# A new order table, engine table and buffer table for a hand-scheduled attention + MoE kernel

## The chip, the cores and the metric

One core of a Trainium2 chip runs the whole program; the metric is device microseconds of that core, the median of several runs. Its engines take instructions from queues of their own, in order, and wait for each other through semaphores: TensorE (PE in the rows, its weight loads PEld), VectorE (DVE), ScalarE (ACT), GpSimd (POOL) and SyncE (SP), whose queue issues all the kernel's DMAs.

## The reference

```python
# q, k, v: (4, 8, 1152, 64) float32; w_in (512, 2048), w_out (2048, 512)
q_pool = q.reshape(B, H, S // 2, 2, D).mean(axis=3)           # 576 queries
scores = (1.0 / np.sqrt(D)) * np.matmul(q_pool, k.transpose(0, 1, 3, 2))
scores = scores - np.max(scores, axis=-1, keepdims=True)
attn = np.exp(scores)
attn = attn / (np.sum(attn, axis=-1, keepdims=True) + 1e-09)
x = np.matmul(attn, v)        # then transposed to (B * 576, 8 * 64) = (2304, 512)
h = x @ w_in
g = np.where(h > 0.0, h, np.exp(np.minimum(h, 0.0)) - 1.0)
out = g @ w_out               # (2304, 512) float32
```

## The kernel before

There are four units of work, one for each batch. In a unit, attention goes over four pairs of heads; each pair has nine steps of 128 queries (four for each head, and one that takes the last 64 queries of both). Numbers that must be exact are split into a high and a low float16 part (`hi`, `lo`), so most products are done as three matmul passes.

One attention step is this chain, each link a task: `scores` (TensorE, L890, L895, L904, into the single score buffer `s` in PSUM); `biggest` (VectorE, L919: scales `s` into a buffer `ep` and takes the extreme of each row); `expo` (ScalarE, L925); `recip` (the row sum's reciprocal); then one of two ways to the transposed weights `pT`. In the 45 steps of unit 0 and of one more pair: `norm_pool` normalises in `ep` (POOL L945, DVE L948 or ACT L951), TensorE transposes (`turn`, L1002) and `out_act` copies to `pT` (ACT L1012, DVE L1015). In the other 99 steps: `phi_act` makes the high half in a buffer `hb` (ACT L973 or POOL L970), `plo` the low half in `ep` (DVE L976), and two DMA transposes (`p_turn`, L982) put both into `pT`. Then `pv` or `pv_split` (TensorE, L1034, L1046) multiplies with V, and `xb` copies the result to `x32` (DVE L1059 and L1061, ACT L1055).

Before a pair's steps come its loads (L586 to L598), `q_sum` (L607, adds the two queries that are pooled, on DVE or POOL), sums of absolute values (ACT L545), a scale, `hi` (ACT L551 or POOL L502) and `lo` (DVE L565 or POOL), and DMA transposes of Q and K (L647, L698). The weights are loaded and decoded through unit 0 (`dec`, DVE L776 to L780; `w_hi`, `w_lo` L803 to L812).

The MoE part of a unit runs in two groups of 256 and 320 tokens: `m1_all` (TensorE L1149), `neg` and `ex` (ACT L1162, L1165), `em` (POOL L1170, ACT L1175 or DVE L1180), `join` (DVE L1185), `gh` (ACT L1199 or POOL L1207), `gl` (POOL L1203 or DVE L1211), `m2_all` (TensorE L1231), `oe` (ACT L1247) and the store. The MoE of one unit is woven into the attention of the next.

All 2788 tasks are first listed; then two tables written out as text say everything about their order. A word of `ORDER` is a task's number and the letter of its engine (p, v, a, g for PE, DVE, ACT, POOL; s for a DMA on SP); instructions are emitted in that order, so it fixes the order on each engine's queue. `SLOTS` gives, for each buffer in turn, which pool and which place in it. Pools that matter here: `s` 1, `ep` 4 (5 more live in `w_out` space in unit 0), `hb` 2, `pT` 2. Waits follow from the order and the buffers. A score step uses TensorE's array whole and then split by rows, `pv` splits it by columns; `Plan.run` turns a score step round when the array is not whole:

```python
for word in ORDER.split():
    t = self.tasks[int(word[:-1])]
    t.eng = engines[word[-1]]
    t.dur, t.emit = t.ways[t.eng]
    if t.eng == "PE":
        if t.modes == ("full", "row") and mode != "full":
            t.modes, t.turned = ("row", "full"), True
        mode = t.modes[1]
    order.append(t)
```

Of the kernel before, what the change touches and what calls it, by code (L numbers as in the profile page):

```python
# [32 lines left out]
0s 1g 2a 3s 5a 6p 7v 8p 9v 343s 344s 369s 349s 354s 23a 345v 10a 12g 24v 11v 371v 35s 31p 33p 29p  # L33
346v 32a 34a 30a 13p 25p 36g 14a 472p 347a 26a 27p 28a 15p 16a 38s 21p 473v 425s 338s 474a 40a 22a
19p 485p 351v 486v 475g 496p 364s 356v 487a 37a 476a 17p 41p 497v 488g 20a 461p 353s 359s 18a 498a
481p 42v 340v 374s 4s 462v 489a 43p 427v 477p 463a 44v 339s 520p 499g 490p 464g 465g 500a 521v 482a
366v 494p 491a 495a 522a 557p 348s 479p 523g 466p 45a 467a 470p 471a 478a 558v 46v 544p 545v 480v
47s 524a 529p 527p 559a 492p 501p 509p 468p 560v 502v 528a 50g 51g 510v 546a 561a 503p 53s 533p
525p 469a 511a 504a 505p 547g 483p 48s 350v 52s 493a 506a 512v 513a 534v 341v 361v 376v 562p 530a
514p 49s 618p 526a 518p 56s 535a 515a 563a 352a 368s 548a 58a 536v 507p 54g 55a 508a 551p 564p 565a  # L40
420s 537g 540p 516p 552a 619v 355v 519a 517a 541a 59p 60v 553p 357a 342a 61p 363s 542p 370v 543a
62v 620a 581p 549p 566p 582v 538p 567v 484a 539a 554a 372a 63g 570p 64v 571v 568p 605p 583a 550v
555p 572a 429s 621v 584v 606v 585a 358s 68g 69g 622g 573v 574a 360v 627p 628a 65s 373s 556a 586p
# [36 lines left out]
2004g 1009a 986s 1983p 155s 1001a 1016v 1023p 977p 2016v 458v 459a 460g 978a 1002v 995p 1003s 2024g  # L80
1004s 1024v 150a 1033p 2041a 2042a 1025a 1026g 1027g 1011s 151v 1010v 2010a 156s 1017a 1012s 2047p
1034v 2043g 1978p 1984p 157a 996a 1018v 2044v 1019a 1035a 2017a 2025g 1028v 1041p 158a 154a 1036v
1042v 2018g 1979a 146s 1021s 1013p 1051p 1014a 1985a 1030s 159p 1020v 2011v 1043a 1029s 1980s 2045g
1044g 1045g 1986s 1022s 160v 2026p 161p 162v 1052v 1037a 2027a 2028a 163a 2096p 2048a 1039s 168a
2029a 1995v 1038v 2049a 2050a 2046g 1047s 164v 2075p 1069p 1070v 1040s 1053a 1031p 2051v 2030v 169g
1061p 1054v 173s 165s 1071a 1032a 1055a 1046v 1048s 2061p 2054p 1062v 2110p 1057s 2031g 2032v 1056v
2076a 2055a 2056a 2077a 2057g 2058v 1087p 1072v 2062a 1063a 2063a 1088v 2064a 1058s 166s 1049p 170s
2052g 2059g 2060g 1064v 1050v 2097a 2098a 1079p 167s 2082p 2099a 2100v 2065v 2078g 1073g 2068p
2053g 2111p 2066a 2101g 1080v 2102g 1074v 1065a 1067s 1089a 1097p 1059p 1076s 1066v 1075s 1090v
1068s 2069a 2070a 1081a 2083a 2084a 2071g 2072v 1082v 2079v 1098v 2067g 1091a 1093s 176s 2073g  # L90
2080g 2081v 2085g 1060v 171g 1092v 2089p 1083a 1105p 1106v 2122p 2123p 1077p 2090a 1123p 2086v
1107a 2091a 2092a 1085s 1094s 1099a 1108g 1109g 1084v 172v 2103p 2087g 2074g 2112p 1110v 1124v
1115p 2104a 2105a 2093v 2106g 1100v 174g 1086s 2107v 1078v 178a 2108g 2109g 177s 1111s 1101a 1095p
1116v 1102v 1112s 1103s 1117a 1118g 1133p 179a 1119g 2116p 1134v 2094g 2095g 1096a 2128v 1104s
1135a 1125a 1141p 1120v 1126v 1121s 1122s 2088g 1142v 1127a 1113p 175a 2124p 1128v 1136v 1129s
1143a 1137a 1130s 1159p 1139s 1160v 1138v 1114a 1144g 1145a 1146v 1161a 1162g 1163g 2117p 1140s
1131p 1132a 2129v 1151p 180p 2130v 1152v 1148s 181v 1147s 1153a 1164v 2113p 2114a 182p 2131p 2132v
183v 1166s 1187p 1188v 2133p 184g 185v 2134v 1165s 2125p 2115s 1154g 1155g 189a 2137a 1169p 1149p
1170v 2138v 1171a 186s 187s 1179p 1172g 1173g 1156v 1158s 1175s 1157s 1180v 1174v 2153p 2139p 1181a
1150a 2126a 2140a 190v 188s 1176s 1182v 2135v 2141a 2142v 2181p 2143v 2154a 1197p 1167p 1189a 1198v  # L100
2144g 1190g 2145g 1191g 2155a 2156v 2157v 1177p 1168v 1205p 1206v 2127s 191s 194s 2182a 1183a 1192v
2136v 1184v 1178v 1207a 1199a 2183a 2184a 2185v 1200v 1208v 192g 1194s 2167p 1185s 2160p 1233p
2158g 2161a 2162a 2168a 195g 1234v 1193s 2174p 1186s 2163a 2164v 1209a 2169a 1210v 2159g 1201a
# [1200 lines left out]
```

## Time and profile before

| what | value |
|---|---|
| median of 3 runs | 794.65 us (794.53 to 795.88) |
| the profiled execution | 793.59 us, its span 791.5 us, so 2.1 us lie around the span |
| TensorE, VectorE, ScalarE, GpSimd busy | 723.1, 642.9, 585.0, 377.7 us |
| mean granted TensorE clock | 0.990 |

The span runs from the first to the last instruction of the program. A busy TensorE is one with a matmul in the array; the time between matmuls that the page counts as busy can still hold short pauses. "A <- B" in a wait means that an instruction of A stood until one of B had ended.

### The profile page before, as it was taken

Reading aid. Unit: us, or ns where it says so; the run is one execution under the profiler, and the core shown is the slowest. Engines: PE = TensorE matmul, PEld = TensorE weight load, DVE = VectorE, ACT = ScalarE, POOL = GpSimd, SP = SyncE. Lnnn points to the kernel's source line nnn. Section 1 sums busy time; section 2 is a strip of 40 time slices with the busy share of each in tenths; the row PEclk is TensorE's granted clock in tenths of the full one; section 3 lists DMA queues with packets and bytes.
Section 4 is the critical chain, followed back from the end, with each engine's and each line's share of the span. In section 5 each row is a group of like instructions: output and inputs, shape, how many; then the busy total and the mean of one; then the engine's idle time right before and its main releaser. Section 6 shows DMA issues by size and latency. Waiting matters only on the chain. (4 is left out here: it accounts for less than half of the span.)

```text
span 791.5 us, 19657 instructions
## 1 busy us (share of the span) xinstructions
PE 723.1 (91%) x7845; PEld 477.0 (60%) x7845; DVE 642.9 (81%) x1147; ACT 585.0 (74%) x987; POOL 377.7 (48%) x411
## 2 busy tenths in 40 slices
PE   2777898999998989999999899998999988999997
PEld 1455666777565655775556565776665545785653
DVE  4999999999997769898889888899797978875330
ACT  3899999999897867577677666878679755682551
POOL 1344455278655745363475463656346344152230
PEclk9699999999999999999999999999999999999999
DMA  6788763718999999997999797699899999655001
GB/s 212 282 230 201 221 195 111 181 32 168 180 193 207 190 189 179 175 202 135 215 200 202 136 221 147 145 172 169 178 173 209 175 187 149 133 98 99 14 1 33
DMA packets 315819, 129.39 MB, mean 163 GB/s; under 512 B 290064, under 2 KB 292112, under 8 KB 315728
## 3 DMA queue, kind: packets, MB, share of 16 engines
q1 hardware_dynamic: 315728, 128.15, 78.7%
q8 instruction: 61, 1.00, 0.5%
q14 instruction: 30, 0.25, 0.1%
HBM read 45.09 MB, written 4.72 MB: 63 GB/s over the span
## 5 line engine op out<-in xcount | busy, mean ns | idle before, releaser
L919 DVE TENSOR_SCALAR_CACHE_REDUCE ep<-s,sm 128x1152 f32<-128x1152 f32 x139 | 196.1, 1411 | 32.2 <-DMA pT<-ep 20.2
L925 ACT ACTIVATE ep<-ep,wk 128x1152 f32<-128x1152 f32 x139 | 174.2, 1254 | 48.4 <-DVE ep L919 36.3
L1149 PE MATMUL r<-x,wi 128*128 128x256 f16 (+1 forms) x1536 | 197.0, 286 | 0.8 <-DVE tmp L1185 0.8
L1231 PE MATMUL r<-wo,g 128*128 128x512 f16 (+1 forms) x864 | 175.6, 380 | 2.5 <-POOL g L1203 2.2
L1149 PEld LDWEIGHTS <-wi 128*128 128x128 f16 x1536 | 147.8, 98 | 41.3 <-issue 4.2
L976 DVE SCALAR_TENSOR_TENSOR ep<-ep,wk,hb 128x1152 f16<-128x1152 f32 x99 | 150.0, 1521 | 16.0 <-POOL hb L970 8.5
L1231 PEld LDWEIGHTS <-g 128*128 128x128 f16 (+1 forms) x864 | 74.2, 100 | 84.4 <-POOL g L1203 3.1
L890 PE MATMUL s<-kT,qT 128*128 128x512 f16 (+3 forms) x480 | 97.0, 334 | 25.2 <-DVE ep L919 16.4
L1046 PE MATMUL r<-pT,v 128*64 128x128 f16 (+1 forms) x2970 | 85.1, 215 | 4.4 <-DMA pT<-ep 3.1
L1046 PEld LDWEIGHTS <-v 128*64 128x64 f16 x2970 | 78.0, 110 | 15.7 <-issue 14.2
L973 ACT ACTIVATE hb<-ep,wk 128x1152 f16<-128x1152 f32 x51 | 63.7, 1252 | 31.6 <-DMA pT<-hb 15.0
L1203 POOL TENSOR_TENSOR g<-tmp,g 128x320 f16<-128x320 f32 (+1 forms) x63 | 67.2, 1072 | 36.7 <-ACT g L1199 35.1
L970 POOL TENSOR_SCALAR hb<-ep,wk 128x1152 f16<-128x1152 f32 x48 | 61.8, 1288 | 45.1 <-DVE wk L934 16.4
L890 PEld LDWEIGHTS <-qT 128*128 128x128 f16 (+1 forms) x480 | 39.2, 101 | 66.9 <-issue 37.6
L1162 ACT ACTIVATE tmp<-r 128x320 f32<-128x320 f32 (+1 forms) x96 | 45.9, 479 | 36.5 <-PE r L1149 34.7
L502 POOL TENSOR_SCALAR wk<-wk 128x1 f32<-128x1 f32 x59 | 23.1, 391 | 102.1 <-ACT ep L925 98.1
L1185 DVE SCALAR_TENSOR_TENSOR tmp<-r,tmp 128x320 f32<-128x320 f32 (+1 forms) x96 | 51.9, 550 | 21.9 <-POOL tmp L1170 15.9
L904 PE MATMUL s<-kT,qT 64*128 64x512 f16 (+1 forms) x320 | 57.6, 396 | 10.3 <-DVE ep L919 9.1
L1165 ACT ACTIVATE tmp<-tmp,us 128x320 f32<-128x320 f32 (+1 forms) x96 | 58.1, 610 | 4.0 <-DVE us L1103 2.3
L1170 POOL TENSOR_SCALAR tmp<-tmp,us 128x320 f32<-128x320 f32 (+1 forms) x40 | 32.3, 809 | 57.6 <-ACT tmp L1165 57.6
L1002 PE MATMUL r<-ident,ep 128*128 128x128 f32 x360 | 53.0, 285 | 4.1 <-POOL ep L945 1.7
L1207 POOL TENSOR_SCALAR g<-tmp 128x320 f16<-128x320 f32 (+1 forms) x43 | 29.3, 686 | 42.7 <-DVE tmp L1185 40.0
(151 smaller groups left out, 1058.7 us busy)
## 6 DMA issues: line engine op xcount, KB each, us to landing
k<-in_k_dram SPq DMA_DIRECT2D x16, 576.0 KB, 5.2
v<-in_v_dram SPq DMA_DIRECT2D x16, 576.0 KB, 5.0
q<-in_q_dram SPq DMA_DIRECT2D x16, 512.0 KB, 4.2
g<-in_moe_w_out_dram SPq DMA_DIRECT2D x15, 512.0 KB, 5.4
g<-in_moe_w_in_dram SPq DMA_DIRECT2D x14, 512.0 KB, 6.4
qT<-qT SPq DMA_DIRECT2D x45, 144.0 KB, 3.0
out_dram<-tmp SPq DMA_DIRECT2D x16, 256.0 KB, 3.1
pT<-ep SPq DMA_TRANSPOSE x99, 3.6
```

The source lines that it names most:

```text
L890: nc.tensor.matmul(s.ap[rows, c, 0:n], pr.qT.ap[:, 0, j, rows], keys[h][c], start=first[c], stop=not first[c] and c < 2, skip_group_check= ...
L904: nc.tensor.matmul(s.ap[rows, c, 0:512], pr.qT.ap[r, 1, j, rows], keys[h][c][r], start=first[c], stop=not first[c], skip_group_check=True,)
L919: nc.vector.tensor_scalar(e_(), s.ap.rearrange("p a b -> p (a b)")[:, 0:S], pr.sm.ap[:, 12:13], None, op0=ALU.mult, op1=ALU.min, accum_out ...
L925: nc.scalar.activation(out=e_(), in_=e_(), func=AF.Exp, bias=nm.ap[:, 0:1], scale=-1.0, accum_out=nm.ap[:, 1:2],)
L970: nc.gpsimd.tensor_scalar(hb.ap, e_(), nm.ap[:, 1:2], 1.0, op0=ALU.mult, op1=ALU.mult)
L973: nc.scalar.activation(out=hb.ap, in_=e_(), func=AF.Copy, scale=nm.ap[:, 1:2])
L976: nc.vector.scalar_tensor_tensor(out=e16(), in0=e_(), scalar=nm.ap[:, 1:2], in1=hb.ap, op0=ALU.mult, op1=ALU.subtract)
L1046: nc.tensor.matmul(half(h), pr.v16.ap[:, h, order[c], e], p, start=(j + c == 0), stop=(j == 2 and c == NCH - 1), skip_group_check=True,)
L1149: nc.tensor.matmul(hp.ap[:, f * n:(f + 1) * n], w_in16[g][:, a, c, (f0 + f) * 128:(f0 + f + 1) * 128], x16.ap[:, e, c, g0:g0 + n], start=( ...
L1165: nc.scalar.activation(out=en.ap[:, :m], in_=en.ap[:, :m], func=AF.Exp, scale=us.ap[:, 8:9])
L1203: nc.gpsimd.tensor_tensor(out=l, in0=gv, in1=h, op=ALU.subtract)
L1231: nc.tensor.matmul(op.ap[r0:r0 + tn, :], gt[qd].ap[:, a, fi, o:o + tn], w_out16(f // 2)[:, e, f % 2, :], start=(i < 128 // tn), stop=(i >= ...
```

## The change

The text of `ORDER` and of `SLOTS` is replaced; nothing else. Both tables are of the same length (2788 words, 1378 places). The pools and the kinds of instruction stay the same. 354 tasks change their engine; counted over both tables, by task and engine:

| task | before | after |
|---|---|---|
| `em` on ACT, DVE, POOL | 35, 21, 40 | 31, 33, 32 |
| `gh` on ACT, POOL | 48, 48 | 46, 50 |
| `gl` on DVE, POOL | 28, 68 | 35, 61 |
| `hi` on ACT, POOL | 23, 20 | 33, 10 |
| `lo` on DVE, POOL | 34, 9 | 37, 6 |
| `norm_pool` on ACT, DVE, POOL | 21, 3, 21 | 15, 4, 26 |
| `out_act` on ACT, DVE | 110, 25 | 115, 20 |
| `phi_act` on ACT, POOL | 51, 48 | 59, 40 |
| `q_sum` on DVE, POOL | 5, 11 | 6, 10 |
| `recip` on DVE, POOL | 85, 59 | 81, 63 |
| `w_hi` on ACT, POOL | 8, 8 | 6, 10 |
| `w_lo` on DVE, POOL | 14, 2 | 11, 5 |
| `xb` on ACT, DVE | 54, 26 | 50, 30 |

On TensorE 103 of 597 tasks keep their rank in the queue, and none moves by more than 17 ranks; on SP 79 of 358 keep it and none moves by more than 24. 751 of the 1378 buffer places differ. The core of the diff, with the first lines of each table and those that hold tasks 1074 and 1098:

```diff
 ORDER = """
-0s 1g 2a 3s 5a 6p 7v 8p 9v 343s 344s 369s 349s 354s 23a 345v 10a 12g 24v 11v 371v 35s 31p 33p 29p
-346v 32a 34a 30a 13p 25p 36g 14a 472p 347a 26a 27p 28a 15p 16a 38s 21p 473v 425s 338s 474a 40a 22a
...
-2053g 2111p 2066a 2101g 1080v 2102g 1074v 1065a 1067s 1089a 1097p 1059p 1076s 1066v 1075s 1090v
-1068s 2069a 2070a 1081a 2083a 2084a 2071g 2072v 1082v 2079v 1098v 2067g 1091a 1093s 176s 2073g
...
+2069a 2070a 1089a 2063a 1059p 1080v 2071g 1073g 1067s 167s 2072v 1090g 1091a 1074v 1105p 1068s
...
+2083a 2084a 2096p 1107a 1097p 1084v 2097a 2073a 1060v 2066g 1098v 2085g 1077p 2122p 2123p 2086v
...
 """
 
 SLOTS = """
-00 00 00 00 00 00 00 00 00 04 00 02 00 04 03 00 00 01 03 01 02 00 00 01 00 01 00 01 00 01 01 00 00
...
+00 00 00 00 00 00 00 00 00 03 00 01 01 03 04 02 00 04 00 01 02 00 00 01 00 02 00 00 00 01 01 00 00
...
 """
 SPLIT = ("ffff", "ssss", "ssfs", "ssss")
```

## Rows read from the trace of the kernel before

**Rows 1.** The page: each engine's busy us, share of the span, instructions.
```profile
PE 723.1 (91%) x7845; PEld 477.0 (60%) x7845; DVE 642.9 (81%) x1147; ACT 585.0 (74%) x987; POOL 377.7 (48%) x411
```

**Rows 2.** Busy time by stretch: stretch, its length, engines' busy us, clock, DMA.
```profile
0.00:20.00 20.00, 5.20 (x28) 2.93 (x29) 8.61 (x21) 7.55 (x11) 2.35 (x8) 1.00 0.62 214
20.00:180.00 160.00, 137.22 (x1380) 101.11 (x1380) 152.89 (x309) 150.51 (x279) 78.71 (x76) 0.96 0.62 179
180.00:720.00 540.00, 514.16 (x5947) 334.65 (x5944) 460.44 (x775) 399.49 (x643) 283.22 (x308) 1.00 0.95 176
720.00:792.00 72.00, 66.51 (x499) 38.35 (x497) 20.96 (x46) 27.44 (x55) 13.43 (x20) 0.98 0.08 23
```

**Rows 3.** Waits of TensorE, 180 to 720: us in total, times, longest.
```profile
PE s L890 <- DVE ep L919: 11.6, 13, 2.4
PE s L904 <- DVE ep L919: 5.5, 7, 1.1
PE r L1046 <- DMA pT<-ep: 3.1, 4, 1.1
...
PE r L1046 <- DMA pT<-hb: 0.9, 1, 0.9
```

**Rows 4.** Tile pT, 180 to 720: who waited for it, and DMA landing times.
```profile
  DVE ep L919: 20.2, 18
...
DMA to landing us min/median/max: 3.2/3.6/6.9
```

**Rows 5.** Timeline around 281: start, duration, instruction, idle time before it.
```profile
279.71 1.41 DVE L976 SCALAR_TENSOR_TENSOR ep<-ep,wk,hb 128x1152 f16<-128x1152 f32 x1
...
281.46 1.59 SPq L982 DMA_TRANSPOSE pT<-ep  x1
...
286.81 1.42 DVE L919 TENSOR_SCALAR_CACHE_REDUCE ep<-s,sm 128x1152 f32<-128x1152 f32 x1 [4.11 <-DMA pT<-ep]
...
288.28 0.65 PE L890 MATMUL s<-kT,qT 128*128 128x512 f16 x3 [2.40 <-DVE ep L919]
```

**Rows 6.** The chain that ended last: start, us, TensorE piece.
```profile
674.17 0.49 PE s L890 x3
...
674.72 0.32 PE s L904 x2
...
675.35 2.70 PE r L1231 x12
...
678.91 5.35 PE r L1149 x48
...
691.47 3.13 PE r L1046 x108
```

**Rows 7.** VectorE's groups by line and shape: busy, mean ns, idle before.
```profile
L565 DVE SCALAR_TENSOR_TENSOR qn<-q,sm,qn 128x576 f16<-128x576 f32 x14 | 15.5, 1105 | 1.2 <-ACT qn L551 1.2
...
L1211 DVE TENSOR_TENSOR g<-tmp,g 128x320 f16<-128x320 f32 x18 | 13.4, 746 | 4.3 <-ACT g L1199 2.5 <-POOL g L1207 1.8
...
L1015 DVE COPY pT<-r 128x384 f32<-128x384 f32 x18 | 9.6, 547 | 0.4 <-PE r L1002 0.4
...
L806 DVE SCALAR_TENSOR_TENSOR wi<-wi,wk,wi 128x1024 f16<-128x1024 f32 x6 | 7.7, 1276 | 0.0
...
L1180 DVE TENSOR_SCALAR tmp<-tmp,us 128x320 f32<-128x320 f32 x14 | 6.3, 449 | 8.6 <-ACT tmp L1165 8.6
...
L607 DVE TENSOR_TENSOR q<-q 128x576 f32<-128x576 f32 x5 | 5.7, 1137 | 4.0 <-DMA q<-in_q_dram 4.0
...
L948 DVE TENSOR_SCALAR ep<-ep,wk 128x1152 f32<-128x1152 f32 x3 | 2.4, 810 | 0.0
...
L1061 DVE COPY x<-r 128x128 f32<-128x128 f32 x4 | 1.1, 276 | 0.0
```

**Rows 8.** ScalarE's groups by line and shape, as in rows 7.
```profile
L951 ACT ACTIVATE ep<-ep,wk 128x1152 f32<-128x1152 f32 x17 | 21.3, 1260 | 2.0 <-DVE wk L934 1.5 <-POOL wk L942 0.6
...
L551 ACT ACTIVATE kn<-k,sm 128x1152 f16<-128x1152 f32 x9 | 11.2, 1244 | 3.3 <-DVE sm L497 3.3
```

More of the change, by code (lines that the diff above doesn't have):

```diff
@@ L38 @@
[L38 to L43, printed above, removed]
@@ new lines @@
+113s 821p 834p 798v 871p 850g 851g 841p 852p 437v 1915v 862a 822a 115a 112a 434s 1918v 853a 436v
+1947p 103s 104s 835a 438a 406v 407v 1926p 1948a 842a 108a 1949a 1950g 397g 408a 109v 863v 864g 854p
+856p 440v 1927a 872v 855a 1928a 857a 1929g 1919p 1951v 843p 441p 114s 442v 884p 398g 1930v 873a
+1920a 1921a 1922a 885v 844v 443p 845p 1933p 874g 116a 117p 886a 846v 1923v 875g 444v 118v 887v
+1934a 897p 1931a 445g 119p 867p 865p 869p 120v 898v 868a 121a 858p 888a 122v 123s 126g 915p 446v
+870a 878p 859v 899a 866a 916v 893p 891p 876p 879a 892a 889p 890a 905p 894a 917a 900v 127g 1987v
@@ new lines @@
+906v 880p 877a 901g 895p 131s 918v 124s 1935a 881a 923p 902v 903s 924v 896a 1952a 1936g 882p 907a
+919g 1924a 883a 129a 1940p 925a 908v 1953v 1925g 447a 1988v 1941a 1942a 1937v 1938a 1989v 920v
+1990p 1991v 1932v 941p 904s 128s 942v 922s 1961p 921s 909a 911s 1962a 1943a 130v 926v 1992p 933p
+134s 448g 910v 1968p 943a 1963a 1964a 132g 912s 927g 934v 1939g 935a 1993v 951p 1996a 1965v 944v
+1944v 928v 929s 1969a 1975p 1954p 936v 1997v 1945g 952v 945a 136a 1970a 946v 449g 1971a 937a 450v
+125s 938v 913p 914a 930s 931p 953a 133a 979p 980v 1955a 1956a 135s 137a 954v 1972v 2033p 948s 959p
@@ new lines @@
+2131p 1164v 1187p 1166s 2132v 2125p 1188v 2133p 185v 1153a 1154g 1155g 2134v 1169p 2137a 1170v
+1149p 2138v 1179p 1189a 2126a 1171a 1172v 1156v 2135v 1150v 194s 2167p 2153p 2146p 186s 195v 189a
+2168a 1173a 1180v 2154a 1181a 1157s 1174v 190v 1190g 2169a 2170g 2171v 2172g 1182v 1191a 1158s
+2115s 1175s 2155a 187s 2156v 2157v 2158g 2139p 1176s 1192v 1167p 1205p 1206v 1183a 2140a 2141a
+2181p 1168a 191s 2159g 2142a 188s 1193s 2143v 2144a 1184v 1207a 1197p 1177p 1198v 2118p 1178a 2182a
+1199a 2183a 2160p 1194s 1185s 2127s 2173g 1233p 2147a 2148a 2145g 1200v 1201g 1202v 1208v 2184g
@@ new lines @@
+2185v 1186s 1209g 2174p 1234v 1195p 1203s 1204s 197s 2149v 1210v 2150v 1215p 2151g 1235a 2161a
+2162a 2175a 192a 1236g 2152g 1211s 2119p 1216v 1212s 193v 2163v 1217a 2176a 1218v 1219g 1221s 1225p
+1226v 1220v 1222s 2120a 2164v 1227a 1228v 2165g 2166g 2177a 2195p 1237a 2178v 1243p 1244v 1213p
+198s 196a 1238v 2196p 2179g 1245a 1196a 199a 2207v 1214v 1251p 1239s 2136v 1223p 1229g 1224a 1240s
+1231s 1252v 2180g 2197p 2208v 1246g 2209v 200a 2121s 201p 1247a 1230v 202v 1269p 2210p 203p 1253a
+1254v 2211v 204v 2188p 210a 1248v 2201p 205g 1249s 2212p 1255a 1232s 1270v 1271a 206v 1250s 2202p
@@ new lines @@
+2226a 2227a 1315p 1316v 2251g 2228v 1302v 2229v 1285s 2254a 1277p 1325p 2206s 223p 224v 2255a 2256a
+1286s 2281p 225g 2309p 2252v 1326v 1278a 1317a 226v 2257v 2267p 1327a 1318g 2310a 1328v 1307p 1319g
+1320v 1303s 1308v 2282a 2283a 2284v 2311a 2312a 2285v 1309a 1329g 2313v 2230a 2258a 2286a 1295p
+1330v 1304s 1305p 2314a 2231g 1333p 237s 2287g 2315g 227s 2288p 1322s 1296v 2268a 1321s 2269a 1334v
+1332s 1331s 228s 2239p 2240a 2241a 2259v 2270v 2271v 2289a 2260p 2272a 2261a 1306v 2262a 1310v
+1335a 2242g 1311g 1343p 2273g 1344v 2232p 2243v 2244g 2263a 2264v 2233a 233s 2234a 2290a 2291a
@@ new lines @@
+1456v 1448g 1411p 1412v 1449g 255g 1431p 1421a 1457a 1458g 1429p 1433p 1434v 1432v 1444s 2340a
+1430a 1463p 1464v 256a 1435p 260a 1450v 1465a 1443s 1451s 1466g 1459a 1452s 1484p 1485v 1486a 261p
+262v 2342p 2343p 1460v 1461s 1487g 1488g 1467a 1436v 1473p 1474v 1475a 1476g 263p 1477g 1453p 2344p
+1468v 1462s 264v 265a 1489p 1493p 1508p 2345p 1491p 1454v 1509v 1494v 266v 1469s 1497p 1470s 1471p
+1498v 1510a 1472v 1521p 1490v 1492a 270a 1522v 1511g 1512g 275s 2341s 1478p 267s 271g 272s 1499a
+1500v 2346a 2348v 1513p 1480p 1501g 2335s 1481a 1517p 1482p 1534p 1479a 1518a 1483a 278s 1523a
@@ new lines @@
+2455a 2447a 2448g 1658s 2449v 317s 2450a 1666a 2451g 2502a 1689v 1650p 2456v 2503a 1659s 1660p
+1651a 309s 1680p 2478a 2479g 2459p 314s 318g 1690a 2516a 1667v 1674a 1669s 1681v 2504a 1698p 2505v
+1668s 2517a 1661v 2460a 1675v 2461a 2506a 2507g 1691g 1676s 1699v 315a 2457a 2458g 1692a 1677s
+1693v 2518g 320s 1682a 2422p 2462v 2519v 2494p 2495a 2496a 2438p 1683v 316v 1695s 1706p 2463v 2423p
+2424p 1707v 2497g 1684g 2464g 1685v 1694s 321s 1716p 2465g 1686s 1678p 2439a 2520a 2521g 1700a
+1701v 2440a 1708a 322a 1717v 2425a 1734p 2508p 1702a 2498v 2499a 2500g 1709g 2441v 2442v 323a 1703v
@@ new lines @@
+1679a 2435v 2443a 319a 2466p 1710a 2444v 324p 2522p 1687s 325v 326p 1711v 2426s 1704s 1705s 310s
+327v 1718a 1719v 2467a 2468a 2529p 1712s 2509a 2510a 2523a 2550p 1735v 2524a 1720g 1724p 1713s
+2511a 328a 2469v 2470v 2471g 2472v 311s 329v 2512v 330s 1696p 1725v 1721v 2525a 1736a 1726a 1697a
+1714p 1737g 1722s 1723s 331s 1738g 1727v 1728g 2513g 333a 1715v 1739v 1744p 1745v 2526v 2536p 1741s
+1729v 2543p 1730s 1770p 2551p 1771v 334v 1731s 1740s 1752p 2544a 2537a 2538a 2545a 2539v 2540v
+1746a 335s 332s 1772a 2546a 2527g 2562p 2528v 1747v 1748a 1753v 2530a 2531a 2541a 2547v 2514v 2532v
@@ new lines @@
+1732p 1749v 2563p 1742p 1750s 1762p 2548g 1751s 1754a 1733a 1755v 1756g 1743a 1758s 2556p 2533v
+1763v 1773v 1757v 1780p 1781v 1764a 1765g 1766a 1767v 1759s 2557p 1768s 1774a 1775v 1769s 1782a
+2534g 1788p 1789v 2564p 2535v 1760p 1790a 2549v 2542g 1806p 1791v 1777s 1776s 1783g 1807v 1792a
+1793v 1808a 1761a 1794s 1784a 2552p 1798p 1795s 1809g 2565p 1799v 1810a 1778p 1785v 1824p 1800a
+1801g 1786s 1787s 1811v 1812s 1825v 2558p 336a 1779v 2568v 1802a 1826a 1813s 1834p 1827g 1828g
+2559p 1803v 1835v 1836a 337v 1816p 1829v 2560a 1804s 1805s 1796p 1814p 1837v 1838g 1830s 1831s
@@ new lines @@
+1817v 1797a 1842p 2561s 1840s 1815v 2569v 2570v 2571p 2572v 2573p 2574v 2566a 2577a 1843v 2578v
+1839v 2553p 1818a 1819v 1820g 2554a 2575v 2555s 1841s 1844a 1862p 1863v 1822s 1845v 1846g 1821v
+2607p 2608a 1864a 2593p 1847v 2594a 2595a 2596g 1852p 1853v 2614p 2597v 1865g 1866g 2600p 1823s
+2567s 2598a 2609a 1848s 1867v 2615a 2616a 2617v 1854a 1898p 2610v 2611v 1832p 1849s 1899v 2618v
+1868s 1850p 1900a 2612g 2619g 2599g 1855v 1870p 1856a 2620g 2601a 1871v 1872a 2579p 1873v 1833v
+1851v 1874a 2580a 1888p 1857v 1869s 2602a 2603a 1875v 1858s 1901g 2581a 2582g 2604v 2605g 2586p
@@ new lines @@
+2587a 2588a 1859s 1889v 1902g 1876s 2628p 2589v 2590v 2591a 1903v 1890a 1891v 2606v 2583v 2621p
+1892a 1877s 2629a 1860p 1861a 2630a 2592g 1878p 2584g 2585g 1904s 2613v 1880p 1881v 1882a 1883v
+2641p 1905s 1894s 1893v 1884a 1885v 1886s 1887s 2622a 2623a 2631g 2632v 2635p 2636p 2637p 2624g
+2633a 1879a 1895s 2625v 1906p 1907a 2626a 1896p 2627g 2647v 2642p 1897a 2648v 2649v 2634v 2650p
+2651v 2638p 2652p 2653v 2656a 2654v 2576v 2639a 2643p 2644p 2645a 2640s 2657v 2686p 2658p 2728p
+2687a 2688a 2689a 2690v 2691a 2729a 2730a 2731g 2732v 2655v 2692g 2659a 2660a 2661v 2662v 2663g
@@ new lines @@
+2664g 2672p 2665p 2666a 2667a 2668a 2669v 2673a 2674a 2675v 2693p 2676v 2677a 2678v 2670g 2646s
+2733a 2671v 2694a 2695a 2696v 2697v 2698a 2699g 2734v 2735p 2700p 2679p 2680a 2681a 2682v 2683v
+2684g 2685g 2736a 2737a 2738v 2739v 2740g 2741g 2763p 2721p 2722a 2723a 2724v 2725v 2726g 2727v
+2701a 2702a 2714p 2703g 2704v 2705a 2706v 2715a 2756p 2742p 2757a 2758a 2759v 2716a 2717g 2760v
+2770p 2776p 2718v 2764a 2765a 2766g 2767v 2768g 2761g 2762v 2719a 2720v 2743a 2744a 2745a 2707p
+2708a 2709a 2710a 2711v 2712g 2713v 2749p 2771p 2772p 2777p 2746v 2747g 2750a 2751a 2752v 2778p
```

237 lines of the change are left out of this document (87 added, 150 removed), and 82 rows, old and new, of the table SLOTS.

## Prediction

> **What bounds the kernel now.** I read the page first. TensorE is busy 91% of the 791.5 us span, VectorE 81%, ScalarE 74%, GpSimd 48% [rows 1]; no engine but TensorE is near its limit on average, so the time is TensorE's work plus its pauses, and an order table can only change the pauses and the small costs between matmuls. The table by stretches says where the pauses lie [rows 2]: 14.8 us in the first 20 us (nothing has landed yet), 22.8 us from 20 to 180, 25.8 us from 180 to 720 (540.0 less 514.16), 5.5 us after that. In the second stretch VectorE is busy 152.9 of 160 us and ScalarE 150.5: there the softmax of unit 0 and the weight decode set the pace, not a landing. In the third, VectorE has 80 us to spare, so a pause there is a matter of order. The TensorE waits of that stretch come next [rows 3]: 17.1 us in 20 pauses of the score matmuls behind `biggest` (L919: the score buffer `s` is single, so the next scores wait until VectorE has read it), and 4.0 us of the `pv` matmuls (L1046) for DMA transposes. Last I asked who waits for the transposed tile's DMA [rows 4]: L919 itself, 20.2 us in 18 waits, because it writes the `ep` buffer that a transpose still reads; a transpose takes 3.2 to 6.9 us from issue to landing, 3.6 in the median. One case whole [rows 5]: `plo` ends at 281.1, the transpose goes out at 281.46, L919 has waited 4.11 us when it starts at 286.81, and TensorE stands 2.40 us. That is what the change aims at.
>
> **What the change leaves alone.** Both tables hold the same 2788 tasks, and buffers of one kind only trade places. The TensorE tail has the same shape: the matmuls behind the last `pv` are the same ones, and their tasks, at the prices of [rows 6], add to 63 us in both. I count it as nothing; its cover is that TensorE work, and if it were gone each elementwise chain of about 3 us would show.
>
> **Part 1, cover for late landings.** I counted in both tables the TensorE work that stands between the task that releases a transpose (`plo` or `phi`) and the task that needs it, and priced it: a score step 1.0 us, a 24-matmul `m1` 2.7 and a 12-matmul `m2` 2.7, a `pv_split` 1.6 [rows 6]. From `plo` to the `pv` that reads it (99 pairs), cover under 6 us falls from 20 cases to 7; from `phi` to `pv` (99) from 8 to 1; from `plo` to the next L919 in the same `ep` buffer (95) from 23 to 12. For the 18 waits of [rows 4] the mean cover grows from 6.4 to 9.6 us and the shortest from 1.0 to 5.2; the L919 of [rows 5], task 1098, goes from 1.9 to 5.2. A landing of 3.6 to 6.9 us plus the wait in SP's queue is what such cover must hide. How much of TensorE's pauses is this? At most all that stands behind L919 and the transposes, 17.1 + 4.0 = 21.1 us [rows 3]; at least the direct 4.0 and the one pause shown, 6.4 us [rows 3, 5]. Going back one step from each of the 20 pauses, about 11 of the 17.1 us come from an L919 that itself waited for a landing, so I take 15. Cases under 6 us fall from 51 to 20, 0.39 of them; a longer cover also moves other cases closer, so I let 0.45 of the 15 us stay: **minus 8 us**, bounds minus 4 (the direct waits alone) and minus 15.
>
> **Part 2, more array switches.** A score step splits the array by rows, a `pv` by columns, the rest uses it whole. In the chain the row pair costs 0.32 us, where three score matmuls of 1152 columns cost 0.49, so that 512 columns would be 0.22: a switch costs 0.10 us [rows 6]. Going through both tables with the kernel's own rule for turning a step round gives 328 switches before and 351 after: 23 x 0.10 = **plus 2.3 us**, with nothing that hides it; lower bound 0 if the pairs fall in pauses that exist anyway. [...]
>
> **Part 3, the saturated start.** Ahead of the 29th `biggest` VectorE gets one normalisation (0.81 us), two `q_sum` (1.14 each), three `xb` (0.28 each) and loses two `out_act` (0.55 each) [rows 7]: plus 2.8 us. One `q_sum` is that of the first pair, at a time when VectorE has nothing to do (8.61 us busy of the first 20 [rows 2]), so plus 1.7. ScalarE loses three normalisations (1.26 each) and three `xb` (0.28) and gains three `hi` passes (at most 1.24 each, those of Q about half) [rows 8]: minus 1 to minus 2. Both engines are full there, so which of them counts changes from step to step; bounds minus 2 and plus 3, I take **plus 1 us**, nearer to VectorE, whose L919 the TensorE waits name.
>
> **Part 4, engine choices over the whole.** 354 tasks change engine. Of VectorE: twelve more `em` (0.45), seven more `gl` (0.75), three more `lo` (1.1 for Q; those of K and V are twice as large, and I take 1.6), one normalisation (0.81), one `q_sum` (1.14), four `xb` (0.28), less five `out_act` (0.55) and three `w_lo` (1.28): 5.4 + 5.2 + 4.3 + 0.8 + 1.1 + 1.1 - 2.8 - 3.8 = 11.3, less four pairs of small reciprocal instructions: some plus 10 us [rows 7]. ScalarE gets eight more `phi_act` and six fewer normalisations (both about 1.26), ten more `hi` and fewer small tasks, about plus 6 [rows 8]; GpSimd loses 21 tasks. Past 180 us VectorE's 80 idle us and ScalarE's 140 [rows 2] hide it: 0. If that cover were gone, it would be the 10 us.
>
> **Sum.** -8 + 2.3 + 1 + 0 = -4.7 us against the profiled execution, 793.59 us (span 791.5 and 2.1 outside it): 788.9. The median of the three runs shown is 1.06 us above that execution, so the forecast is **790.0 us** against 794.65.
>
> **The rivals.**
> *The cover is bought, little comes back* (0.17). Only the direct 4.0 us go [rows 3]; L919 is late anyway because VectorE's queue is, as in about a third of its 20 pauses. -4.0 + 3.3 = -0.7: 794.0. For it: another order of issues on SP makes other transposes late than those that the old trace shows. Against it: the shortest covers grew all over the table, not only in the 18 places.
> *VectorE takes the place of the landings* (0.25), slower. The 10 us more on VectorE end up ahead of `biggest`, the instruction that 17.1 us of pauses already stand behind [rows 3], and GpSimd's lower load does not help, as it was idle half the time. Price: +10 + 2.3 + 1.7 - 4.0 = +10.0: 804.7 at worst; with half of the 10 us exposed, 799.7. It decides once VectorE passes some 95% busy beyond 180 us, as it is before that. For it: the start already runs like that, and VectorE's queued work ahead of the last score steps, by the same prices, grows against TensorE's by about 8 us. Against it: 80 us of slack in that stretch.
> *All late pauses go* (0.10). -15 + 2.3 - 2 = -14.7: 780.0. Against it: one landing takes up to 6.9 us [rows 4], and 20 covers stay under 6.
>
> **How the numbers follow.** The forecast has 0.48, the larger gain 0.10, the small one 0.17, the slower one 0.25. A measurement of this kernel tells about 0.2%, 1.6 us, from no change. Faster by more: 0.48 + 0.10 = 0.58; within: 0.17; slower: 0.25. The likeliest case's own range is 784 to 793 (cover -13 to -4 and the start -2 to +3). To leave out no more than 2 in 10, the range drops most of the largest gain and the outer part of the slower case: 783 to 800.
>
> **What would show it.** Right: L919's waits for the transposed tile fall from 20.2 us to under 10, the `pv` waits from 4.0 to about 1, TensorE's pauses from 180 to 720 from 25.8 to about 18, its busy time up by some 2 us, and those of 20 to 180 about the same. Part 2 is wrong if TensorE's busy time stays at 723; part 3 if VectorE's idle time in the start, not its work, changes. The prediction is wrong if the waits for landings fall and pauses behind L919 stay (VectorE's queue, the slower rival), or if new waits for DMA turn up at other tiles: loads of K, V and weights, whose cover I found no longer than before (K loads with under 6 us: 8 before, 10 after).

## The result and the profile after

The changed kernel takes **775.03 us** (median of 4 runs, 774.34 to 775.73) against 794.59 us (4 runs) of the kernel before: 0.9756 of its time, 95% interval 0.9733 to 0.9779, or 19.6 us less. The forecast was 790.0 us and its range ended at 783: the direction was right, the size less than a quarter of what came.

The profiled execution after took 775.73 us, with a span of 773.6 us and a mean granted clock of 0.998. Lines of the kernel after are one higher than before (L919 is now L920, L1046 L1047). First the page's line of engines, which answers to [rows 1]:

```profile
PE 723.4 (94%) x7845; PEld 476.6 (62%) x7845; DVE 637.3 (82%) x1160; ACT 590.5 (76%) x992; POOL 359.9 (47%) x394
```

TensorE's busy time is the same, 723.4 us; on the page the whole gain is in its pauses, 50.2 us (773.6 less 723.4) where there were 68.4. The table by stretches of the kernel after, as in [rows 2]:

```profile
0.00:20.00 20.00, 4.68 (x31) 3.42 (x32) 9.29 (x21) 8.63 (x14) 0.99 (x7) 1.00 0.70 240
20.00:180.00 160.00, 138.94 (x1380) 100.34 (x1380) 151.53 (x313) 148.53 (x277) 82.67 (x76) 0.99 0.66 183
180.00:720.00 540.00, 531.11 (x6135) 344.72 (x6132) 461.32 (x794) 412.33 (x661) 263.35 (x290) 1.00 0.97 175
720.00:774.00 54.00, 48.70 (x311) 28.16 (x309) 15.21 (x34) 21.02 (x44) 12.91 (x21) 0.99 0.04 13
```

From 180 to 720 us TensorE pauses 8.9 us instead of 25.8, in the same 540 us. Its waits in that stretch, as in [rows 3]:

```profile
PE s L891 <- DVE ep L920: 2.1, 2, 1.9
...
PE s L905 <- DVE ep L920: 1.5, 3, 0.8
```

3.6 us in 5 pauses behind `biggest`, where there were 17.1 in 20, and no row in which `pv` waits for a transpose (4.0 before). Who waits for the transposed tile's DMA, as in [rows 4]:

```profile
  DVE ep L920: 3.9, 4
...
DMA to landing us min/median/max: 3.2/3.6/6.8
```

The transposes take as long as before; `biggest` waits for them 3.9 us instead of 20.2. That is the picture that the prediction drew, only more of it. What it didn't foresee lies in the start. Here is the stretch up to the end of the 32nd `biggest`, first before, then after (columns as in [rows 2]; that end is at 146.1 and at 143.0):

```profile
0.00:146.10 146.10, 109.72 (x1063) 77.61 (x1063) 129.99 (x258) 125.52 (x228) 61.32 (x67) 0.95 0.68 202
```
```profile
0.00:143.00 143.00, 108.86 (x1029) 76.00 (x1029) 125.74 (x260) 122.92 (x223) 60.85 (x63) 0.99 0.72 209
```

VectorE needs 4.3 us less, ScalarE 2.6 less, to get there, where part 3 of the prediction had VectorE with more work ahead of the 29th. And VectorE's total fell by 5.6 us, where part 4 had it rise by 10.

### The profile page after: what moved, and what is told of

It is laid out like the page before. It is cut to its first block, busy times and chain, and to the rows that moved or that the text cites. A ratio compares the mean times of both kernels' runs of the same rounds, so it can differ in the third digit from the quotient of the medians.

```text
span 773.6 us, 19674 instructions
## 1 busy us (share of the span) xinstructions
PE 723.4 (94%) x7845; PEld 476.6 (62%) x7845; DVE 637.3 (82%) x1160; ACT 590.5 (76%) x992; POOL 359.9 (47%) x394
## 5 line engine op out<-in xcount | busy, mean ns | idle before, releaser
L920 DVE TENSOR_SCALAR_CACHE_REDUCE ep<-s,sm 128x1152 f32<-128x1152 f32 x140 | 197.6, 1412 | 23.6 <-PE s L905 14.6
L1232 PE MATMUL r<-wo,g 128*128 128x512 f16 (+1 forms) x888 | 181.3, 380 | 2.2 <-POOL g L1204 1.6
L977 DVE SCALAR_TENSOR_TENSOR ep<-ep,wk,hb 128x1152 f16<-128x1152 f32 x99 | 145.6, 1473 | 9.3 <-POOL hb L971 4.7
L1232 PEld LDWEIGHTS <-g 128*128 128x128 f16 (+1 forms) x888 | 76.1, 100 | 88.5 <-issue 4.2
L974 ACT ACTIVATE hb<-ep,wk 128x1152 f16<-128x1152 f32 x59 | 73.7, 1250 | 24.2 <-POOL wk L943 11.1
L503 POOL TENSOR_SCALAR wk<-wk 128x1 f32<-128x1 f32 x63 | 21.4, 339 | 136.5 <-ACT ep L926 135.1
L1047 PE MATMUL r<-pT,v 128*64 128x128 f16 (+1 forms) x2970 | 84.6, 215 | 0.2 <-DVE v L566 0.2
L1047 PEld LDWEIGHTS <-v 128*64 128x64 f16 x2970 | 78.0, 110 | 11.0 <-issue 9.6
L971 POOL TENSOR_SCALAR hb<-ep,wk 128x1152 f16<-128x1152 f32 x40 | 59.1, 1477 | 37.8 <-DVE wk L935 13.0
L1204 POOL TENSOR_TENSOR g<-tmp,g 128x320 f16<-128x320 f32 (+1 forms) x57 | 61.9, 1093 | 28.5 <-ACT g L1200 26.9
L1003 PE MATMUL r<-ident,ep 128*128 128x128 f32 x369 | 56.3, 287 | 7.9 <-POOL ep L946 1.9
L1171 POOL TENSOR_SCALAR tmp<-tmp,us 128x320 f32<-128x320 f32 (+1 forms) x32 | 24.9, 778 | 83.0 <-ACT tmp L1166 81.8
L1003 PEld LDWEIGHTS r<-ident,ep 128*128 128x128 f32 x369 | 40.9, 144 | 19.3 <-issue 5.5
## 6 DMA issues: line engine op xcount, KB each, us to landing
qT<-qT SPq DMA_DIRECT2D x45, 144.0 KB, 2.8
```

Source lines behind the costliest of these rows:

```text
L920: nc.vector.tensor_scalar(e_(), s.ap.rearrange("p a b -> p (a b)")[:, 0:S], pr.sm.ap[:, 12:13], None, op0=ALU.mult, op1=ALU.min, accum_out ...
L971: nc.gpsimd.tensor_scalar(hb.ap, e_(), nm.ap[:, 1:2], 1.0, op0=ALU.mult, op1=ALU.mult)
L974: nc.scalar.activation(out=hb.ap, in_=e_(), func=AF.Copy, scale=nm.ap[:, 1:2])
L977: nc.vector.scalar_tensor_tensor(out=e16(), in0=e_(), scalar=nm.ap[:, 1:2], in1=hb.ap, op0=ALU.mult, op1=ALU.subtract)
L1003: nc.tensor.transpose(tp.ap[:, c * 128:(c + 1) * 128], e_()[:, (j + c) * 128:(j + c + 1) * 128], ident)
L1047: nc.tensor.matmul(half(h), pr.v16.ap[:, h, order[c], e], p, start=(j + c == 0), stop=(j == 2 and c == NCH - 1), skip_group_check=True,)
```

## The experiments

The theory that I tested (A) is that of the prediction with a larger size: late landings stand behind nearly all pauses past 180 us, also behind those that I had put down to VectorE's queue. Rivals: (B) landings are worth about 8 us and a better order of the other work the rest; (C) the engine choices matter. All times are medians; the kernel before took 794.0 to 795.3 us beside them.

**Engine letters and order, each alone.** The first has the order of after with the engine letters of before (354 words change their letter), the second the order of before with the letters of after. One word of the first, out of its line:

```diff
-... 2071g 1073g 1067s 167s 2072v 1090g 1091a ...
+... 2071g 1073g 1067s 167s 2072v 1090v 1091a ...
```

> The order and the buffers of after, with the engine of every task as it was before the change (354 tasks go back). Theories A and B: most of the gain stays, 775 to 783 us. Theory C: the gain goes with the engines, 788 to 795 us.

Measured: 856.23 us, ratio 1.0773 (1.0731 to 1.0815).

> The order and the buffers of before, with the engine of every task as after the change. Theories A and B: no gain, 790 to 797 us, since covers and landings are those of before. Theory C: 776 to 783 us.

Measured: 864.94 us, ratio 1.0898 (1.0871 to 1.0926). Every theory missed: either half alone costs some 60 to 70 us. Over the whole span, score matmuls wait 35.5 and 48.0 us for `biggest`, against 29.0 in the kernel before; TensorE's pauses in all are 105.9 and 114.0 us against 68.4, and it is busy 754.0 and 748.7 us, at mean granted clocks of 0.961 and 0.969. The largest of these waits, over the whole span, in the kernel before and in the second of the two (whose line numbers are one lower):

```profile
PE s L890 <- DVE ep L919: 16.4, 20, 2.4
PE s L904 <- DVE ep L919: 9.1, 10, 1.9
```
```profile
PE s L889 <- DVE ep L918: 24.9, 26, 3.0
PE s L903 <- DVE ep L918: 19.6, 14, 3.4
```

What follows is only that order and engines are one plan; a likely reason, not tested by itself, is that a task given to an engine at a place that was chosen for another holds up that queue. Such a cross tells nothing about what either half is worth inside its own plan, so C is not refuted by it; the next runs go at the landings, and answer C too.

**Without the transposes.** The first try:

> The kernel before, without the transposing DMAs of the softmax tiles (both halves, all 99 pairs of tiles): the places that they fill are set once to a constant and read as they are, so the products behind them are not the reference's. Everything else, orders, engines, buffers, stays. No `pv` and no L919 waits for such a landing any more, and the DMA engines are lighter. Theory A (late landings stand behind nearly all pauses past 180 us, also behind those that I had put down to VectorE's queue): 773 to 778 us, TensorE's pauses from 180 to 720 fall from 25.8 to under 9 us. Theory B (landings are worth the 8 us of the prediction, the rest of the gain is a better order of the other work): 785 to 788 us, pauses of 16 to 18 us. Theory C (it is the engine choices): 788 to 792 us.

> The kernel after the change with the same transposing DMAs left out and the same constant in their place. Theory A: little is left to gain, 771 to 775 us, so that the gap to the kernel before with the same cut is under 4 us. Theories B and C: it stays 9 us or more ahead of the kernel before with the same cut, 771 to 776 against 785 to 792 us.

Measured: 856.88 us (1.0792, 1.0761 to 1.0823) and 870.44 us (1.0970, 1.0923 to 1.1017). These two kernels did more than their expectations say: they set the place anew each time it was taken, and GpSimd paid for it (GpSimd's groups of the first):

```profile
L372 POOL MEMSET pT<- 128x2304 f32 x75 | 151.1, 2019 | 17.2 <-PE r L1050 6.6 <-PE r L1038 6.3 <-ACT wo L957 2.6
...
L372 POOL MEMSET x<- 128x4608 f16 x9 | 35.4, 3938 | 4.1 <-PE r L1038 4.1
```

186.5 us of added GpSimd work hide what was asked, so they say nothing on landings. The second try adds no instruction (the core of its edit):

```diff
...
+place = (pT.tag, pT.slot, st.h or 0, j)
+if place in turned_once:
+    return
+turned_once.add(place)
 nc.sync.dma_start_transpose(
...
```

> The kernel before, with 174 of its 198 transposing DMAs of softmax tiles left out: each place of the transposed tile is filled once (24 transposes) and read again as it is, so the products behind the other 174 are not the reference's. No instruction is added this time; orders, engines and buffers stay. Theory A (late landings stand behind nearly all pauses past 180 us, also those I put down to VectorE's queue): 773 to 778 us, TensorE's pauses from 180 to 720 fall from 25.8 us to under 9. Theory B (landings are worth the 8 us of the prediction, the rest of the gain is a better order of the other work): 784 to 788 us, pauses of 15 to 18 us. Theory C (each order table hangs together, and landings are a small part of it): 788 to 793 us.

Measured: **777.21 us**, 0.9792 (0.9770 to 0.9814).

> The kernel after the change with the same 174 transposing DMAs left out. Theory A: little is left to gain, 770 to 775 us, and the gap to the kernel before with the same cut is under 4 us. Theories B and C: it stays 9 us or more ahead of the kernel before with the same cut.

Measured: **771.88 us**, 0.9728 (0.9703 to 0.9754). Theory A's times, but the gap between the two is 5.3 us, where it had under 4. In the kernel before, without transposes, the pauses behind `biggest` shrink to this (TensorE's waits, 180 to 720; L927 is its `biggest`):

```profile
PE s L898 <- DVE ep L927: 3.7, 5, 1.3
PE s L912 <- DVE ep L927: 3.5, 4, 1.3
```

From 17.1 to 7.2 us, in the old order with the old engines: so 9.9 of those 17.1 us were landings, and TensorE's pauses of the stretch fall from 25.8 to 12.1 (540 less the 527.91 of its row by stretches), nearer to A's "under 9" than to B's 15 to 18, but inside neither. Without its transposes a `pv` no longer waits for the softmax either; it made no use of that, for in this trace no `pv_split` began less than 2.1 us after the end of its last `plo` (2.3 in the kernel before, 55 cases), so what was gained is the landing. These two kernels also keep the places of the transposed tile as fixed tiles, so a control has that edit alone:

> Control for the runs without transposes: the kernel before with all 198 transposes, but with the places of the transposed tile kept as two fixed tiles instead of a new tile for each use, as those runs had them. If the keeping by itself costs nothing, 793 to 796 us; if part of the 17.4 us that the run without transposes gained came from it, under 790 us.

Measured: 793.76 us, 0.9980 (0.9962 to 0.9998). It is worth 1.2 us, by the interval 0.2 to 3.0, and not the 17.4.

**Start and rest apart.** The two orders were joined behind the first 705 tasks: `ORDER` has the first 705 words of one kernel, then all other words in the order of the other. The places are dealt by the rule that both tables of before and after follow already (every place that is taken again is the one that came free first), so the table of places follows from the order and is no change by itself.

> The first 705 tasks (the first 180 us) in the order and on the engines of after, all others as before; buffers dealt anew, least recently used first. The two sets of 705 tasks differ in 5 tasks each way. Theory of the traces (the start is worth 1 to 2 us of the 19, the stretch from 180 us on the rest): 790 to 794 us. Rival (what the start leaves behind, loads further ahead and a better filled queue, carries the gain): under 783 us.

Measured: 793.55 us, 0.9990 (0.9966 to 1.0015).

> The first 705 tasks (the first 180 us) in the order and on the engines of before, all others as after; buffers dealt anew. Theory of the traces: 775 to 779 us, the gain stays. Rival (the start carries it): 788 us or more.

Measured: 779.81 us, 0.9829 (0.9808 to 0.9851), 0.8 above the range of the first theory and far from the rival. The rest brings 14.8 us by itself; the start brings 4.8 more in front of it (779.8 to 775.0), but only 1.0 in front of the old rest. To place the 5.3 us, the second of these kernels ran without transposes too:

> The first 180 us in the order of before, all else in the order of after, and 174 of the 198 transposing DMAs of softmax tiles left out as in the two runs with 777.2 (before) and 771.9 us (after). It places the 5.3 us between these two, which no landing explains. Theory S (they lie in the start): 775.5 to 778 us. Theory R (they lie in the order of the other work past 180 us): 771 to 773.5 us.

Measured: 777.12 us, 0.9771 (0.9746 to 0.9796). Theory S. All medians in one table:

| first 180 us | rest | all transposes | 174 left out | they cost |
|---|---|---|---|---|
| before | before | 794.6 | 777.2 | 17.4 |
| before | after | 779.8 | 777.1 | 2.7 |
| after | after | 775.0 | 771.9 | 3.1 |

Read the column without transposes downwards: past 180 us the two orders are then equal (777.2 and 777.1), so all that the new order and the new engines gain there is cover for landings, 17.4 less 2.7; theory C has nothing left past 180 us. The start is worth 4.8 and 5.2 us with transposes and without: it is another thing.

**Which wait.** The transposes stay, but read a tile that nobody writes any more:

```diff
-out=p16(j).rearrange("p (c s) -> p c s", c=NCH), in_=e16() if j else hb.ap
+out=p16(j).rearrange("p (c s) -> p c s", c=NCH), in_=w_in16[0].rearrange("p a k f -> p (a k f)")[:, 0:S]
```

> The kernel before, with every one of the 198 transposing DMAs kept at its size, place and destination, but reading a weight tile that lies still instead of `hb` and `ep`: the load of the DMA engines stays, while no `biggest`, no `phi` and in effect no `pv` waits for a landing any more (what is transposed, and so the products behind it, are not the reference's). Waits theory (a landing costs because somebody stands and waits for it): 775 to 780 us, as with the transposes left out (777.2). Load theory (leaving the transposes out helped because the DMA engines had half the work): 786 to 794 us.

Measured: 783.46 us, 0.9852 (0.9824 to 0.9879).

> As the run before it, but only the 99 transposes of the low halves read the weight tile; those of the high halves read `hb` as in the kernel before. So `biggest` waits for no landing, while `phi` still waits for that of `hb`, and `pv` for the high half. If the wait of `biggest` is nearly everything: 776 to 781 us. If the chain over `hb` (15 us of waits each on ScalarE and GpSimd) and `pv` carry a third or more: 783 to 788 us.

Measured: 787.92 us, 0.9916 (0.9891 to 0.9940).

> The kernel after the change with all 198 transposes kept, but reading the weight tile that lies still, so that `ep` and `hb` are never held by a landing. The same edit gave the kernel before 11.8 us. Cover theory: little is left here, 771 to 775 us. If after still pays for the sources as before did: under 768 us.

Measured: 772.25 us, 0.9712 (0.9686 to 0.9739). Of the 17.4 us, some 7 hang on `biggest` waiting for `ep`, some 4 to 5 on the chain over `hb`, and 5 to 6 remain with the sources free. The waits for `hb` stand in the trace before, on ScalarE and GpSimd (180 to 720):

```profile
ACT hb L973 <- DMA pT<-hb: 15.0, 10, 2.7
```
```profile
POOL hb L970 <- DMA pT<-hb: 15.7, 7, 5.9
```

The expectations missed the middle: neither the waits theory nor the load theory had 783, and the second of these runs ended in the range that gives `hb` and `pv` a third or more. What remains is waiting as well (waits of TensorE, then of SP's queue, in the first of the three, 180 to 720):

```profile
PE r L1046 <- DMA pT<-wi: 5.5, 7, 1.6
...
PE s L904 <- DMA kT<-kn: 1.4, 1, 1.4
PE s L890 <- DMA qT<-qT: 1.3, 1, 1.3
```
```profile
SPq L982 <- PE r L1046: 21.0, 8, 4.9
```

I had written that in effect no `pv` waits any more; but a transpose still goes out only when its place in `pT` is free (SP stands 21.0 us behind the `pv` that reads it), and `pv` waits 5.5 us for the landing. Whether a lighter DMA load by itself lands anything sooner isn't separated by these runs. In the kernel after, free sources bring 2.8 us, against 11.8 before.

**Cover taken away.** Only the places of `ep` are dealt anew. The edit is to words of `SLOTS`; the rule that deals them, in words:

```diff
-s = min(free_places, key=came_free)     # the place that came free first
+s = max(free_places, key=came_free)     # the place that came free last
```

> Order and engines of after; only the four `ep` places are dealt in another way: each new tile takes the place that came free last instead of the one that came free first. Ends of use with under 2 us of TensorE work, by the kernel's own task costs, before the next use grow from 23 to 66 of 137 (32 in the kernel before). Cover theory: the waits of `biggest` for landings come back, 790 to 810 us. Rival (the order of the engines is good whichever place a tile lies in): under 779 us.

Measured: 876.62 us, 1.1030 (1.0997 to 1.1064).

> The kernel that took the most recently freed `ep` place (876.6 us), with the transposes of the low halves reading a weight tile that lies still, so that no `biggest` waits for a landing (what is transposed is not the reference's). If its 100 us come from landings that `biggest` waits for: under 800 us. If they come from the places being taken too soon behind other users (`plo` itself, TensorE's transposes): over 840 us.

Measured: 793.22 us, 0.9972 (0.9949 to 0.9995). VectorE's waits of these two, over the whole span, the first with landings and the second without:

```profile
DVE ep L920 <- DMA pT<-ep: 84.2, 34, 5.6
```
```profile
DVE ep L920 <- PE s L905: 16.3, 18, 3.0
DVE ep L920 <- PE r L1003: 15.1, 10, 3.2
```

Same order, same engines: 101.6 us lost by the places alone, and 83.4 of them come back when `biggest` has no landing to wait for (some 30 of the 101.6 are TensorE's own work at a mean granted clock of 0.959 instead of 0.998, as the last section shows). The other 18 go with waits such as that for TensorE's transposes (L1003). The direction of theory A, far over the size that it gave.

**The price of a switch.**

```diff
-if t.modes == ("full", "row") and mode != "full":
+if False and t.modes == ("full", "row") and mode != "full":
```

> The kernel after the change without its rule for turning a score step round: every half step runs its row part last, so that the switches of the array between row, column and whole use grow from 351 to 384; the same matmuls otherwise. With the price of the prediction's part 2, 0.10 us for each: TensorE's busy time or its small gaps grow by 3.3 us in all, 778 us. If a switch costs nothing here: 774 to 776 us and the same busy time.

Measured: 776.00 us, 0.9764 (0.9741 to 0.9787), and TensorE busy 726.6 us. One of the 34 steps concerned, in the timeline of TensorE (start, us, instruction), first as it is after the change, then without the turn:

```profile
318.71 0.39 PE L905 MATMUL s<-kT,qT 64*128 64x512 f16 x2
319.03 0.66 PE L891 MATMUL s<-kT,qT 128*128 128x512 f16 x3
319.53 0.22 PE L896 MATMUL s<-kT,qT 128*128 128x128 f16 x1
319.59 0.93 PE L1150 MATMUL r<-x,wi 128*128 128x256 f16 x7
```
```profile
318.70 0.66 PE L891 MATMUL s<-kT,qT 128*128 128x512 f16 x3
319.20 0.22 PE L896 MATMUL s<-kT,qT 128*128 128x128 f16 x1
319.35 0.39 PE L905 MATMUL s<-kT,qT 64*128 64x512 f16 x2
319.67 0.83 PE L1150 MATMUL r<-x,wi 128*128 128x256 f16 x6
```

From the step's first matmul to the next task's first: 0.88 us with one switch, 0.97 with two. In the median of the 34 steps the difference is 0.094 us. The busy time grew by 3.1 us (726.6 less 723.4), where 0.10 apiece gives 3.3; but this profile ran its 20 to 40 us at a granted clock of 0.72, that of after at 0.98, so part of the 3.1 can be the clock's. The median grew by 1.0 us, less than these runs can tell from nothing. So the time is that of a switch that costs nothing, the single steps are those of 0.10: TensorE's pauses fell from 50.2 to 47.3 us (773.9 less 726.6), and most of the added busy time took their place.

## Why the prediction was right or wrong

**What bounds the kernel: right.** TensorE's work plus its pauses; the pauses past 180 us moved, the busy time did not.

**Where the 15.0 us lie.** Between the forecast and the result, 6.7 us lie in part 1, 5.8 in part 3, and 2.3 in part 2, whose cost did not show in the time. With part 1 alone at its measured size the forecast would have been 783.3, just inside the range; it took part 3 as well to leave it. The range was also drawn too narrow: the bounds that the prediction gives for cover and start (-13 to -4, -2 to +3), with the 2.3 of the switches, run from 782 to 796, not from 784 to 793.

**Part 1, the step that failed first.** The mechanism was right and its size was not: minus 8 us was forecast, about minus 14.7 came (17.4 less 2.7). Both factors of that term were off, the second far more:
- "I take 15" as the share of the pauses that are landings. Transposes cost the kernel before 17.4 us (16.6 against the control). Not that all 17.1 us behind `biggest` were landings: 7.2 of them stay without transposes, so 9.9 were, near the 11 that the prediction had counted. I missed the chain over `hb`, which the tile's row for `biggest` alone does not show [rows 4], and which is worth 4 to 5 us.
- "I let 0.45 of the 15 us stay". 2.7 of 17.4 stay, 0.16, as the waits themselves do (3.9 us of 20.2 + 4.0). I had scaled with the number of covers under 6 us, 20 of 51, and put something on top. A count gives a cover that is 0.1 us short the weight of one that is 5 us short, and the change lengthened the shortest most. Summing by how much each cover falls short of 4 us, a little over the median landing, gives by the same tables and prices 24.8 us before and 6.4 after, 0.26: nearer, at no more work. The 4 us were chosen with the result known, and no other change has tried them.

**Part 2, right in size, not in effect.** A switch takes 0.094 us, where the prediction had 0.10, and in the pair without transposes TensorE is busy 722.0 us after against 719.6 before, 2.4 us more, at clocks of 0.991 and 0.988. That the page's busy time stayed at 723, which was to show part 2 wrong, doesn't show it: in the profile before TensorE ran its 20 to 40 us at a granted clock of 0.66 (1.00 up to 24 us, 0.50 from 25 to 38), and after at 0.98, so its busy times there are not the same measure. But "nothing that hides it" was wrong: past 180 us the new order has 16 of the 23 switches, 1.6 us by this price, and without transposes the two orders take the same time there (777.2 and 777.1); in the experiment most of the added busy time took the place of pauses. Why a switch takes the time that it takes, these runs don't show.

**Part 3, wrong in sign, the second step that failed.** Plus 1 us was forecast, minus 2 to plus 3 its bounds; the start is worth minus 4.8. I had counted which optional tasks change engine ahead of the 29th `biggest`, and neither which fixed ones move behind it nor that durations change. Up to the 32nd, VectorE has one decode tile less (a piece each of L776, L777 and L780), two `out_act` and one pass of L1087 less; at the durations of before these only cancel the additions (0.2 us more in all). That VectorE needs 4.3 us less comes from shorter instructions: L776 takes 0.44 us in the mean of this stretch instead of 0.48, L780 0.69 instead of 0.73, L565 0.95 instead of 1.04. What shortens them there, with GpSimd as busy as before (60.9 us after, 61.3 before), stays open, and that VectorE's work sets the pace of the start is read from its share, not tested. The clock, 0.95 and 0.99 in the rows above, is not the reason: with the old start and 1.00 from 20 to 40 us (the second joined kernel) the 32nd `biggest` ends at 147.4, with the new start and 0.72 (after without transposes) at 142.6. Behind the old rest the lead is lost near the joint: in the profile of the first joined kernel the 32nd `biggest` ends at 144.0, 2.1 us ahead of the kernel before, and the 40th at 187.1, 1.1 us behind it. What the joint costs, and so what the start would be worth there without it, isn't shown.

**Part 4, zero was nearly right, for the wrong reason.** I had plus 10 us on VectorE, hidden by idle time. VectorE's busy time fell by 5.6 us. The count of tasks was right: at the durations of before it gives 9.9 us more. But durations are not fixed, and shorter ones took back more than that: `plo` before and after, by VectorE's groups:

```profile
L976 DVE SCALAR_TENSOR_TENSOR ep<-ep,wk,hb 128x1152 f16<-128x1152 f32 x99 | 150.0, 1521 | 16.0 <-POOL hb L970 8.5 <-ACT hb L973 7.5
```
```profile
L977 DVE SCALAR_TENSOR_TENSOR ep<-ep,wk,hb 128x1152 f16<-128x1152 f32 x99 | 145.6, 1473 | 9.3 <-POOL hb L971 4.7 <-ACT hb L974 4.1
...
L1212 DVE TENSOR_TENSOR g<-tmp,g 128x320 f16<-128x320 f32 x25 | 12.4, 507 | 5.1 <-POOL g L1208 3.5 <-ACT g L1200 1.6
```

`plo` is 48 ns shorter in the mean, `gl` goes from 0.75 us [rows 7] to 0.51 on 320 columns, and seven more of them cost less in all than before. The rival in which VectorE takes the place of the landings rested on those 10 us; it fell with them. The rival of all late pauses going was nearest, at 780.0: its pauses did go (14.7 us of its 15), the start brought 4.8 where it had 2, and the 2.3 of the switches did not show.

## What to carry to other kernels

Price a change of order by how far each cover falls short of the landing, summed, not by how many covers are short (nearer here, in one case), and over every buffer that the transfer holds: its source places, the intermediate one and its destination. Count moved tasks with the durations of the trace, but expect these to move too (`plo` by 48 ns in the mean here). Leaving the transfers out of both kernels, with nothing added, tells in two runs how much of a gain is cover; dealing one pool's places the other way tells how much hangs on them. An order and its engine choices are one plan: half of one with half of the other measured over 60 us worse than either and explained nothing.

## What the runs showed of the hardware

**`plo` ran longer beside GpSimd's work.** In the trace before, `plo` takes 1.41 us in the mean when GpSimd is busy for under a tenth of it (41 of 99) and 1.59 when GpSimd is busy for over 0.8 of it (27 of 99); after, 1.41 (48) and 1.61 (20). `biggest`, which reads PSUM, takes 1.41 either way. Not all of GpSimd's work went with a longer `plo`: in the first kernel without transposes, 21 `plo` ran beside nothing but GpSimd's `MEMSET`s, and 20 of them took 1.40 to 1.43 us. GpSimd worked 17.8 us less after the change, and 21 tasks moved off it. That the one is the cause of the other is read from the overlap, not from an experiment, and what makes `plo` longer isn't shown.

**How a landing depends on the load stays open.** With 24 transposes in place of 198 the DMA engines' share from 180 to 720 us fell from 0.95 to 0.37 (the first row, the kernel before without 174 transposes), and the median of the transposes that were left is 3.4 us from issue to landing, against 3.6. But those that were left lie from 185 to 204 us and from 471 to 526, where the engines were nearly as busy as ever (the other two rows), so these runs say little about a light load:

```profile
180.00:720.00 540.00, 527.91 (x6137) 343.65 (x6135) 468.96 (x793) 403.29 (x649) 284.89 (x309) 1.00 0.37 82
```
```profile
180.00:200.00 20.00, 19.38 (x207) 15.19 (x205) 18.66 (x38) 18.66 (x28) 15.29 (x12) 1.00 0.84 176
...
480.00:520.00 40.00, 37.73 (x504) 29.16 (x500) 34.75 (x59) 28.39 (x50) 26.41 (x29) 1.00 0.85 158
```

**A lower clock came with more pauses.** In the kernel with the `ep` places dealt the other way the same 7845 matmuls kept TensorE busy 753.6 us instead of 723.4, at a mean granted clock of 0.959 instead of 0.998: of the 101.7 us that its span grew, 30 are TensorE's own work, longer at the lower mean clock, the other 71 pauses. Three of its stretches:

```profile
180.00:200.00 20.00, 16.06 (x167) 12.05 (x166) 17.32 (x33) 13.00 (x27) 13.22 (x10) 0.83 0.37 83
...
320.00:340.00 20.00, 16.67 (x200) 10.07 (x199) 16.12 (x20) 13.10 (x22) 12.86 (x17) 1.00 0.99 193
...
380.00:400.00 20.00, 20.00 (x289) 14.84 (x288) 14.63 (x23) 13.20 (x22) 10.59 (x11) 1.00 1.03 177
```

In the stretch without pauses the clock was at 1.00; with about as many pauses it was at 0.83 in one stretch and at 1.00 in another, so the rows show a lower clock together with pauses, not what brings it.
